# Attention and a mixture of experts on one core: the first expert's first range grows from 256 to 384 rows, and a batch's gating moves into the attention

## The chip, the cores and the metric

The kernel runs on one NeuronCore of a Trainium2 chip. The metric is the device time of one execution in microseconds (us); lower is better. The engines are TensorE (PE, with its weight loads shown as PEld), VectorE (DVE), ScalarE (ACT), GpSimd (POOL) and SyncE (SP, which only issues transfers).

## The reference

Three stages follow each other. Everything is float32.

```python
# attention: q, k, v of 4 batches x 8 heads x 576 positions x 64; a window of 64 positions
scores = where(0 <= rel < 64, scale * q @ k.T, -1e9); out = softmax(scores) @ v
x = out.transpose(0, 2, 1, 3).reshape(2304, 512)
# experts: 8 of them, each token goes to two
noisy = x @ w_gate + log1p(exp(x @ w_noise)) * noise
for the two largest of each row, with weights softmax(those two):
    out[row] += weight * (relu(x[row] @ w1[e]) @ w2[e])     # 512 -> 1024 -> 512
# a last dense layer on all rows: 512 -> 2048 -> 512
g = h * clip(h + 3, 0, 6) / 6 with h = out @ w_in;  result = g @ w_out
```

## The kernel before, in words

**Attention.** 16 pairs of heads (`n` = 0 to 15, four pairs to a batch), each in three groups of query chunks, are 48 steps `g` of one software pipeline. The order on TensorE is written by hand; DVE, ACT, POOL and SP are ordered by the scheduler when the program is built. A step turns the exponentials (`pt`), makes the scores (`s`) of a later group, and multiplies with the values (`pv`); DVE takes the maxima (`mx`) and writes the normalised rows to `xbuf` (`normalise`). `load_pair(n + 3)` fetches a later pair's q and k (`rq`, `rk`) and v; a transfer waits, on SP, for one issued eight before it.

**Gating.** The 2304 tokens are 18 tiles of 128; they become known batch by batch (`DONE`: tiles 0-3, 4-8, 9-12, 13-17). `gate_batch` gives a list of steps for one batch: `turn_tile` (four transposes of a tile, and its rows to DRAM, `x_rows`), `logits`, `logits_back`, `s1` to `s5` (the noise, the two largest, their one-hot masks `mk`, and each token's place in its expert's list), then per tile `runs` (two pairs of one-hot matrices `pa` and `pbt` on DVE) and `mms` (their products on TensorE), and `total`, which adds the products to the lists (`iacc`). In the attention these steps hang in the list `fill`, and `bg` places a few of them in each step `g`.

**The first expert early.** After `KNOWN` batches, `hold` copies the first columns of the lists to `idx0`; `gather(0, m)` fetches 128 rows each on POOL, and `build(0, m)` turns them (`xg` to `xh`, `xl`: each float32 matrix is a high and a low part, so one product is three matmuls). An expert works in two ranges of rows (`expert_sub(e, 0)` and `(e, 1)`): 8 column groups of hidden products `ph`, 12 matmuls each, then for each block of 128 rows 24 matmuls `py`. `put(f, ...)` hangs a step between these matmuls: the tables `when` and `when_late` hold the places, 0 to 31 behind each three `ph` matmuls, from 32 on behind each three `py` matmuls.

**Weights.** `Halves.step` loads a weight tile (`wraw`, two buffers), makes the high half (POOL or ACT), and one step later `settle` makes the low half on DVE. The first expert's eight tiles are stepped in the attention, at the end of pairs 5, 6, 7, 9, 10, 11, 13, 14 and 15; the second expert's in the first expert's second range.

Of the kernel before, what the change touches and what calls it, by code (L numbers as in the profile page):

```python
# [29 lines left out]
CAP = 5  # L30
LIM = CAP * 128
SUBS = ((0, 2), (2, CAP))

HOLD = SUBS[0][1] * 128
KNOWN = 2

BASE = 1024
NEG = -1.0e30
# [7 lines left out]
def attention_moe_kernel(ctx, tc, q, k, v, w_gate, w_noise, noise, w1, w2, w_in, w_out, out):  # L46
# [47 lines left out]
    first_part = gp.tile([128, 1], F32, name="first_part")  # L94
    dve.tensor_copy(first_part, ident[:, 0:1])

    idx0 = consts.tile([128, SUBS[0][1]], I32, name="idx0")
    idx4 = consts.tile([128, 4, E, CAP], I32, name="idx4")
    rows4 = consts.tile([128, 4, NT, 2], I32, name="rows4")
    gates4 = consts.tile([128, 4, NT, 2], F32, name="gates4")  # L100
# [219 lines left out]
    def gate_batch(ts, bank):  # L320
# [149 lines left out]
        if t0 + n == NT:  # L470
            chain = firsts + [logits, logits_back, s1, s1b, s2, s3, s3b, s4, s5]
            return (chain + [lambda i=i: runs(i) for i in range(n)] + [lambda i=i: mms(i) for i in range(n)] +
                    [total, weigh, piece_rows])
        chain = [("tr", f) for f in firsts] + [("col", logits)]
        chain += [(None, f) for f in (None, logits_back, s1, s1b, s2, s3, s3b, None, None, s4, None, s5)]
        for i in range(n):
# [2 lines left out]

    def hold():  # L480

        dve.tensor_copy(idx0, iacc[:, 0:SUBS[0][1]])
        pc = gps.tile([128, 512], F32, name="g")[:, 0:1]
        pe.matmul(pc, ones, macc[:, 0:1], start=True, stop=True)
        h = gp.tile([128, 1], F32, name="held")
        dve.tensor_scalar(h, pc, -1.0, float(HOLD), op0=OP.mult, op1=OP.add)
        dve.tensor_scalar(h, h, 0.0, first_part, op0=OP.max, op1=OP.mult)
        dve.tensor_tensor(macc[:, 0:1], macc[:, 0:1], h, op=OP.add)
# [12 lines left out]
    def gather(e, m):  # L501
        if e == 0:
            t = XG[e, m] = mp.tile([128, DM], F32, name="xg", bufs=4)
            early = m < SUBS[0][1]
# [34 lines left out]

    def build(e, m):  # L540
        if e == 0:
            s = int(m >= SUBS[0][1])
            turn_rows(XG[e, m], *columns(e, s), 128 * (m - SUBS[s][0]))
# [104 lines left out]
    fill, late, coming = [], [], []  # L648

    def bg(*kinds, n=1):  # L650

# [6 lines left out]
    with tc.manual_schedule(engines={mybir.EngineType.PE}):  # L658
        for which in ("rq", "rk"):
            for a in range(2):  # L660
                tr_half(0, which, a)
        scores(0)
        odd_slots(1)
        scores(1)
        exps(0)

        for g in range(NG + 2):
            n, j = divmod(g, 3)
            for past in ((g - 3, g - 2) if g > 2 and g % 2 else ()):
                normalise(past)  # L670
                m, jj = divmod(past, 3)
                b, p = divmod(m, HP)
                if p == HP - 1 and jj == 2 and b < B - 1:
                    t = gate_batch(DONE[b], lambda: gps.tile([128, 512], F32, name="g"))
                    if b == B - 2:
                        cut = [f for _, f in t].index(None) + 5
                        t, late = t[:cut], [f for _, f in t[cut:] if f]
                    coming += t
                    if b == KNOWN - 1:
                        coming += [(None, None), (None, hold)]  # L680
                        coming += [(None, lambda m=m: gather(0, m)) for m in range(SUBS[0][1])]
                        coming += [(None, None)] * 2
                        coming += [("tr", lambda m=m: build(0, m)) for m in range(SUBS[0][1])]
            bg(None, "tr" if j == 0 else None)
            if g < NG:
                transposes(g)
            if g + 1 < NG:
                exps(g + 1)
            if g < NG:
                pt_copy(g)  # L690
            if g == 0:
                for which in ("rq", "rk"):
                    for a in range(2):
                        tr_half(1, which, a)
            elif j:
                which = ("rq", "rk")[j - 1]
                tr_half(n + 2, which, 0)
                tr_half(n + 2, which, 1)
            if g + 2 < NG:
                scores(g + 2)  # L700
            if g and g % 2 == 0:
                values(g - 2, g - 1)
                bg("col", n=2)
            fill += coming
            del coming[:]
            bg(None, "tr")
            if j == n % 2:
                load_pair(n + 3)
                if n == 1:
                    for w, s in ((w_gate, 0), (w_noise, E)):  # L710
                        for a in range(4):
                            sp.dma_start(wg[:, a, s:s + E], ap_of(w, 32 * a * E, [[128 * E, 4], [E, 32], [1, E]]))
            if j == 2:
                odd_slots(n + 2)
                if n in (5, 6, 7, 9, 10, 11, 13, 14, 15):
                    w0q.step()
        while fill:
            bg(None, "tr", "col", n=len(fill))
    order = ctx.enter_context(ExitStack())
    order.enter_context(tc.manual_schedule())  # L720

# [146 lines left out]

    def expert_sub(e, s, at):

        m0, m1 = SUBS[s]


        if e == 0:
# [61 lines left out]
    NF = F2 // 128  # L936
    three = consts.tile([128, 1], F32, name="three")
    dve.memset(three, 3.0)
    Y, table = {}, None

    def fetch(t, i):

# [20 lines left out]
    for e in range(E):  # L963
# [6 lines left out]
        wq = Halves(expert_weights(e + 1) if e + 1 < E else w_ins + w_outs)  # L970
        if e == 0:
            t = gate_batch(DONE[B - 1], lambda: eps.tile([128, 512], F32, name="py", bufs=2))
            t += [lambda m=m: gather(0, m) for m in range(A1, M)] + [lambda m=m: build(0, m) for m in range(A1, M)]

            when = [0, 1, 3, 5, 7, 10, 12, 12, 13, 14, 16, 18, 28, 28, 30, 31, 31, 32, 33,
                    36, 37, 38, 39, 40, 40, 41, 44, 40, 40, 40, 45, 46, 47]
            when_late = [2, 3, 14, 14, 24, 24, 25, 26, 27, 30]
            assert len(when) == len(t) and len(when_late) == len(late)
            for i, f in list(zip(when_late, late)) + list(zip(when, t)):
# [18 lines left out]
        expert_sub(e, 0, at)  # L998

        at.clear()  # L1000
        if e == 0:
            gating.close()
            wpool[1] = pool_of(ctx, "w1")
            fourth.append(pool_of(ctx, "fourth", space=PSUM))
            narrow = ctx.enter_context(ExitStack())
            nar = pool_of(narrow, "narrow")
            wq.fetch()
            nq.fetch()
        elif 1 < e < 5:
            for f in range(8):  # L1010
                put(lambda: next(table, None), "f", f, 1)
        if e == 5:
            for _ in table:
                pass
        if e + 1 < E:
            for m, f, late in ((0, 0, ("f", 6, 0)), (1, 2, ("m", A1, 1)), (2, 4, ("m", A1 + 1, 0))):
                put(lambda m=m: gather(e + 1, m), "f", f, 0)
                put(lambda m=m: build(e + 1, m), *late)
            if e == 0:
                for key in (("f", 1, 1), ("f", 3, 0), ("f", 4, 1), ("f", 6, 1), ("m", A1, 1), ("m", A1, 3),  # L1020
                            ("m", A1 + 1, 2), ("m", A1 + 2, 1)):
                    put(wq.settle, *key)
            for key in ((("f", 1, 0), ("f", 2, 1), ("f", 4, 0), ("f", 5, 1), ("f", 7, 1), ("m", A1, 2),
                         ("m", A1 + 1, 1), ("m", A1 + 1, 3)) if e == 0 else
                        (("f", 1, 1), ("f", 5, 0), ("m", A1, 0), ("m", A1 + 1, 1), ("m", A1 + 2, 0))):
                put(wq.step, *key)
            if e:
# [226 lines left out]
```

## Time and profile before

| | us |
|---|---|
| three runs | 1005.97, 1006.91, 1008.25 (median 1006.91) |
| the profiled execution: its time | 1005.52 |
| its span | 1003.7 |
| TensorE busy | 981.5 (98%) |
| VectorE, ScalarE, GpSimd busy | 567.7, 465.5, 325.9 |
| attention, up to the first `ph` matmul | 0 to 131.88 |
| first expert, to the second's first `ph` matmul | 131.88 to 204.76 |
| experts 2 to 8 and the dense layer | the rest |

TensorE's busy time counts instructions that overlap, so 98% doesn't say that it ran at its peak; what it waited for is read from the gaps in its timeline, and its clock from the column PEclk (1.00 is 2.4 GHz, 0.50 is 1.2 GHz).

### The profile page before, as it was taken

What the parts mean: (1) busy time and instruction counts of PE and PEld (TensorE: products, weight loads), DVE (VectorE), ACT (ScalarE), POOL (GpSimd) and SP (SyncE); (2) the same over time, 40 slices, a digit from 0 to 9 for tenths busy, and PEclk for the clock granted to TensorE, in tenths of its full rate; (3) what the DMA queues carried; (4) which work ended last, traced back from release to release, by engine and by line L of the source; (5) the groups of instructions that cost most, each with busy time, mean ns of one, the idle gap of its engine ahead of it and who ended that gap; (6) DMA issues with size and microseconds to landing.
All of it is one profiled execution on the core that took longest, in us unless ns stands there. A gap on an engine that the chain in (4) does not pass through costs nothing.

```text
span 1003.7 us, 17393 instructions
## 1 busy us (share of the span) xinstructions
PE 981.5 (98%) x6422; PEld 890.8 (89%) x6422; DVE 567.7 (57%) x1398; ACT 465.5 (46%) x1034; POOL 325.9 (32%) x351
## 2 busy tenths in 40 slices
PE   8989989999999999999999999999999999999998
PEld 7988877998988989999998988989988998899997
DVE  5587974666777686666666656435233433344322
ACT  6877742444444444544454446434333433334333
POOL 2132203732425343232421276732344234410000
PEclk9999998999999999999999999999999999999999
DMA  9997432636666566656666463200111002100000
GB/s 170 188 230 196 120 117 69 188 122 202 202 185 205 183 184 186 201 171 207 201 202 198 150 204 117 70 23 27 48 32 48 24 25 64 28 27 22 11 11 24
DMA packets 116394, 122.42 MB, mean 122 GB/s; under 512 B 69840, under 2 KB 78288, under 8 KB 116304
## 3 DMA queue, kind: packets, MB, share of 16 engines
q1 hardware_dynamic: 96144, 86.17, 31.0%
q0 software_dynamic: 9488, 19.94, 7.1%
q10 hardware_dynamic: 10672, 15.15, 4.1%
q8 instruction: 51, 0.84, 0.3%
q14 instruction: 39, 0.32, 0.1%
HBM read 92.91 MB, written 28.31 MB: 121 GB/s over the span
## 4 chain that ended last, share of the span: by engine, by line
PE 86%; DVE 6%; DMA 3%; ACT 2%; issue 1%; SPq 0%; POOL 0%; ACTq 0%; DVEq 0%
PE ph L892 7%; PE ph L894 7%; PE ph L893 7%; PE ph L1193 6%; PE ph L1191 6%; PE ph L1192 6%; PE py L912 5%; PE py L914 5%; PE py L913 5%; PE py L1214 5%; PE py L1213 5%; PE py L1212 5%; PE s L239 2%; PE pv L285 2%; PE pt L255 2%; PE tr L1212 1%
## 5 line engine op out<-in xcount | busy, mean ns | idle before, releaser
L512 POOL DMA_INDIRECT xg<-x_rows,idx x140 | 145.8, 1041 | 221.3 <-DVE xt L523 169.4
L948 POOL DMA_INDIRECT xg<-y_rows,rows x144 | 144.9, 1006 | 222.0 <-DVE xg L956 77.0
L1196 DVE SCALAR_TENSOR_TENSOR g<-g,ph 128x384 f32<-128x384 f32 (+1 forms) x112 | 55.7, 497 | 158.7 <-ACT g L1195 154.6
L1195 ACT ACTIVATE g<-ph,three 128x384 f32<-128x384 f32 (+1 forms) x112 | 60.0, 536 | 100.7 <-PE ph L1193 97.7
L900 DVE SCALAR_TENSOR_TENSOR hl<-ph,hh 128x320 fp32r<-128x320 f32 (+2 forms) x128 | 61.0, 487 | 76.1 <-ACT hh L899 76.1
L1201 DVE TENSOR_TENSOR hl<-g,hh 128x384 fp32r<-128x384 f32 (+1 forms) x112 | 56.2, 502 | 58.9 <-ACT hh L1199 56.1
L899 ACT ACTIVATE hh<-ph 128x320 fp32r<-128x320 f32 (+2 forms) x128 | 54.3, 436 | 67.0 <-PE ph L894 63.8
L1199 ACT CAST hh<-g 128x384 fp32r<-128x384 f32 (+1 forms) x112 | 52.4, 467 | 63.8 <-DVE g L1196 63.8
L517 ACT CAST xh<-xt 128x512 fp32r<-128x512 f32 (+1 forms) x60 | 33.5, 570 | 81.7 <-DVE xt L523 81.3
L518 DVE TENSOR_TENSOR xl<-xt,xh 128x512 fp32r<-128x512 f32 (+1 forms) x60 | 37.2, 630 | 39.8 <-ACT xh L517 39.8
L247 ACT ACTIVATE pb<-s,mx 128x128 f32<-128x128 f32 x144 | 42.4, 369 | 10.7 <-DVE mx L241 7.2
L239 PE MATMUL s<-kt,qbd 128*128 128x128 f32 x288 | 39.9, 275 | 0.2 <-ACT kt L226 0.2
L239 PEld LDWEIGHTS s<-kt,qbd 128*128 128x128 f32 x288 | 38.4, 191 | 0.8 <-ACT kt L226 0.5
L241 DVE TENSOR_REDUCE mx<-s 128x3 f32<-128x384 f32 x48 | 26.6, 554 | 21.5 <-PE s L239 16.1
L523 DVE STREAM_TRANSPOSE xt<-xg 128x512 f32<-128x512 f32 x53 | 37.4, 706 | 0.4
L156 POOL TENSOR_SCALAR vt<-vt 64x520 f32<-64x520 f32 (+1 forms) x32 | 19.2, 600 | 53.4 <-DMA vt<-in_v_dram 30.2
L751 DVE SCALAR_TENSOR_TENSOR na<-mag,raw 128x256 f32<-128x256 f32 x64 | 26.8, 420 | 12.1 <-DMA w_out<-na 5.1
L748 ACT ACTIVATE mag<-raw 128x256 f32<-128x256 f32 x64 | 27.5, 430 | 12.5 <-DVE na L757 12.4
L757 DVE CUSTOM_DVE_ANT_0 na<-mag,nr 128x512 uint16<-128x512 uint16 x64 | 27.3, 426 | 9.1 <-DVE mag L756 0.5
L920 ACT COPY y<-py 128x512 f32<-128x512 f32 x33 | 19.3, 584 | 28.1 <-PE py L914 20.6
L756 DVE SCALAR_TENSOR_TENSOR mag<-na,mag 128x256 int32<-128x256 int32 x64 | 27.3, 426 | 2.2
L285 PE MATMUL pv<-vt,ptb 128*64 128x65 f32 x640 | 26.2, 225 | 2.2 <-DVE xbuf L304 2.2
(517 smaller groups left out, 3174.4 us busy)
## 6 DMA issues: line engine op xcount, KB each, us to landing
wraw<-in_moe_w_dram SPq DMA_DIRECT2D x60, 512.0 KB
y_rows<-y ACTq DMA_DIRECT2D x40, 256.0 KB
raw<-in_moe_w_in_dram SPq DMA_DIRECT2D x32, 256.0 KB
raw<-in_moe_w_out_dram SPq DMA_DIRECT2D x32, 256.0 KB
rq<-in_q_dram SPq DMA_DIRECT2D x32, 144.0 KB
rk<-in_k_dram SPq DMA_DIRECT2D x32, 144.0 KB
x_rows<-xbuf SPq DMA_DIRECT2D x18, 256.0 KB
out_dram<-y ACTq DMA_DIRECT2D x17, 256.0 KB
```

What stands on the lines that cost most here:

```text
L239: pe.matmul(s[:, i, :], l, KT[n][:, k0:k0 + 128], start=False, stop=(i == 2))
L512: pool.indirect_dma_start(out=t[:, i], out_offset=None, in_=pieces(xrows), in_offset=bass.IndirectOffsetOnAxis(ap=idx4[:, i, e, m:m + 1], ...
L892: pe.matmul(p, wh[:, fs], xh[:, d, :n], start=(d == 0), stop=False)
L893: pe.matmul(p, wh[:, fs], xl[:, d, :n], start=False, stop=False)
L894: pe.matmul(p, wl[:, fs], xh[:, d, :n], start=False, stop=(d == 3))
L900: dve.scalar_tensor_tensor(hl[f][:, cs], p, 0.0, hh[f].bitcast(F32)[:, cs], op0=OP.max, op1=OP.subtract)
L948: pool.indirect_dma_start(out=g[:, r], out_offset=None, in_=pieces(left), in_offset=bass.IndirectOffsetOnAxis(ap=rows4[:, r, tt, j:j + 1], ...
L1191: pe.matmul(p, wh[:, c], xh[:, d, :n], start=(d == 0), stop=False)
L1192: pe.matmul(p, wh[:, c], xl[:, d, :n], start=False, stop=False)
L1193: pe.matmul(p, wl[:, c], xh[:, d, :n], start=False, stop=(d == 3))
L1195: act.activation(g, p, AF.Relu, bias=three)
L1212: pe.matmul(py[i], gh[f][:, ms], wh[:, ws], start=(f == 0), stop=False)
```

## The change

The first expert's ranges are now 384 and 256 rows (`FIRST`), and `KNOWN` is 3, so the first range takes rows from tiles 0 to 12. The third batch's gating, of which steps from `s1` on stood between the first range's matmuls, now runs wholly in the attention, with several steps to a place; from pair 12 on each step `g` has one place more. Behind the attention stand the fourth batch's transposes and logits, what is left of `fill`, and the three builds, all ahead of the first range. The first expert's weights are stepped earlier, at pairs 2, 3, 4, 5, 8, 9, 10, 11 and 15. The second expert's weights start between the first range's `py` matmuls. Cut to its core:

```diff
+FIRST = ((0, 3), (3, CAP))
+HOLD = FIRST[0][1] * 128
+KNOWN = 3
...
+        if t0 + n == DONE[KNOWN][0]:
+            return ([("tr", f) for f in firsts] +
+                    [("col", logits)] + [(None, f) for f in (None, logits_back, lambda: (s1(), s1b()), s2,
+                                                             lambda: (s3(), s3b()), None, s4, None, s5,
+                                                             lambda: (runs(0), weigh()))] +
+                    [(None, lambda i=i: (mms(i - 1), runs(i))) for i in range(1, n)] + [(None, last)])
...
-                    if b == B - 2:
-                        cut = [f for _, f in t].index(None) + 5
-                        t, late = t[:cut], [f for _, f in t[cut:] if f]
...
+                        coming += [(None, hold), (None, lambda: [gather(0, m) for m in range(FIRST[0][1])])]
...
+            if n >= 4 * KNOWN:
+                bg(None)
...
-                if n in (5, 6, 7, 9, 10, 11, 13, 14, 15):
+                if n in (2, 3, 4, 5, 8, 9, 10, 11, 15):
                     w0q.step()
...
+            early = len(DONE[B - 1]) + 1
+            for f in t[:early]:
+                f()
+            while fill:
+                bg(None, "tr", "col", n=len(fill))
+            for m in range(FIRST[0][1]):
+                build(0, m)
...
+            t = t[early:] + [lambda m=m: gather(0, m) for m in range(FIRST[0][1], M)] + [change]
+            t += [lambda m=m: build(0, m) for m in range(FIRST[0][1], M)]
+            t += [wq.step, wq.settle] * 4
+            when = [2, 2, 4, 6, 8, 10, 16, 16, 20, 21, 22, 24, 25, 25, 27, 29, 31, 33, 33, 34, 36, 34, 34, 37, 44, 46,
```

TensorE's order from the last full set of value products to the first hidden product, before (`tr<-ident,xg` is a build, `tr<-ident,xbuf` a tile's transposes, `g<-xT,wg` the third batch's logits):

```order
L285 MATMUL pv<-vt_147,ptb 64x65 x14
L532 MATMUL tr<-ident,xg 128x128 x4
L255 MATMUL pt<-ident,pb 128x128 x3
...
L285 MATMUL pv<-vt_148,ptb 64x65 x12
L316 MATMUL tr<-ident,xbuf 128x128 x4
L338 MATMUL g<-xT,wg 32x128 x16
L892 MATMUL ph<-xh_2400,hwa 128x256
```

And in the change (`g<-mk` and `g<-macc` count places, `g<-pbt,pa` are the one-hot products, `py<-xT,wg` the fourth batch's logits):

```order
L286 MATMUL pv<-vt_147,ptb 64x65 x14
L339 MATMUL g<-xT,wg 32x128 x16
L348 MATMUL g<-ident,lt 128x128
...
L394 MATMUL g<-mk,before 128x8
L256 MATMUL pt<-ident,pb 128x128 x3
...
L431 MATMUL g<-pbt,pa 128x144
L317 MATMUL tr<-ident,xbuf 128x128 x8
L491 MATMUL g<-macc,ones 128x1
L317 MATMUL tr<-ident,xbuf 128x128 x12
L339 MATMUL py<-xT,wg 32x128 x16
...
L539 MATMUL tr<-ident,xg 128x128 x12
L893 MATMUL ph<-xh_2714,hwa 128x384
```

The whole of the third batch's lists, the three builds and the fourth batch's five tiles now stand between the attention's last full set of value products and the first hidden product; the third batch's own four tiles stand ahead of this piece.

DVE's order in the change, at the third batch's places in the last steps of the attention (`mk` the masks, `lza` the low half of the first expert's last weight tile, `posn` to `qf` the places):

```order
L385 TENSOR_TENSOR mk<-oh 128x32
L454 TENSOR_SCALAR gw<-gw 128x4
L397 TENSOR_REDUCE msum<-mk 128x8
...
L398 TENSOR_TENSOR macc<-macc,msum 128x8
L407 TENSOR_TENSOR oh<-oh,g 128x64
L592 TENSOR_TENSOR lza<-wraw,hza 128x1024
L408 TENSOR_REDUCE posn<-oh 128x8
...
L415 SCALAR_TENSOR_TENSOR qf<-blkn,posn 128x8
L423 TENSOR_SCALAR pbt<-iotab,cf,tokid 128x144 x2
L422 TENSOR_SCALAR pa<-iota_127,qf 128x128 x3
```

`lza` stood between normalisations before, and now stands inside the chain of the places. Behind the eight pairs of one-hot matrices come the last normalisations, then `iacc` and `idx0`.

SP's order from pair 5's loads on, in the change (`wraw` are quarter tiles of the first expert's weights; before, one `rq` of pair 6 stands where the first `wraw` stands here, and the rest of pair 6 and all of pair 7 where the seven stand):

```order
L170 DMA rq<-in_q_dram 96x6x64 x2
L170 DMA rk<-in_k_dram 96x6x64 x2
L574 DMA wraw<-in_moe_w_dram 32x1024
L173 DMA vt_146<-in_v_dram 128x4x64 x2
L175 DMA vt_146<-in_v_dram 64x2x64
L574 DMA wraw<-in_moe_w_dram 32x1024 x7
L170 DMA rq<-in_q_dram 96x6x64 x2
L170 DMA rk<-in_k_dram 96x6x64 x2
```

Pair 6's first load is now the sixteenth transfer from pair 5's first; it was the fifth.

## Rows read from the trace of the kernel before

**Rows 1.** The page: busy time of the engines.
```profile
PE 981.5 (98%) x6422; PEld 890.8 (89%) x6422; DVE 567.7 (57%) x1398; ACT 465.5 (46%) x1034; POOL 325.9 (32%) x351
```

**Rows 2.** Windows: stretch, length, busy of PE, PEld, DVE, ACT, POOL (instructions), PEclk, DMA, GB/s.
```profile
60.00:100.00 40.00, 35.99 (x496) 32.80 (x493) 32.88 (x120) 29.18 (x87) 11.42 (x16) 1.00 0.82 205
```

**Rows 3.** Windows of 2 us at and in the first range, same columns.
```profile
132.00:134.00 2.00, 2.00 (x18) 2.00 (x19) 0.28 (x1) 0.76 (x2) 0.00 (x0) 1.00 1.04 377
...
146.00:148.00 2.00, 0.43 (x4) 0.22 (x2) 1.93 (x14) 0.00 (x0) 0.00 (x0) 1.00 0.00 0
148.00:150.00 2.00, 1.43 (x8) 1.10 (x9) 1.93 (x12) 0.00 (x0) 0.00 (x0) 0.79 0.00 0
150.00:152.00 2.00, 2.00 (x24) 1.81 (x24) 1.73 (x9) 0.38 (x1) 0.00 (x0) 0.50 0.00 0
...
156.00:158.00 2.00, 2.00 (x11) 1.63 (x10) 0.00 (x0) 0.00 (x0) 0.00 (x0) 1.00 0.00 0
```

**Rows 4.** Timeline, PE, 121 to 205: start, length, instruction, idle before and what ended it.
```profile
121.52 1.15 PE L285 MATMUL pv<-vt,ptb 128*64 128x65 f32 x28
...
131.88 0.38 PE L892 MATMUL ph<-xh,hwa 128*128 128x256 f32 x1
...
148.05 0.61 PE L430 MATMUL g<-pbt,pa 128*128 128x144 f16 x2 [1.62 <-DVE pbt L422]
...
166.78 0.65 PE L532 MATMUL tr<-ident,xg 128*128 128x128 f32 x4 [0.61 <-DMA xg<-x_rows,idx]
...
171.82 0.45 PE L893 MATMUL ph<-xl,hwa 128*128 128x384 f32 x1 [0.28 <-DVE xl L518]
...
188.40 0.39 PE L912 MATMUL py<-hwb,hh 128*128 128x512 f32 x1
...
204.76 0.30 PE L892 MATMUL ph<-xh,hsa 128*128 128x320 f32 x1
```

**Rows 5.** Timeline, DVE and PE, 67 to 71.
```profile
67.15 1.22 DVE L585 TENSOR_TENSOR lxa<-wraw,hxa 128x1024 fp32r<-128x1024 f32 x1
70.67 0.69 PE L285 MATMUL pv<-vt,ptb 128*64 128x65 f32 x16 [1.60 <-DVE xbuf L304]
```

**Rows 6.** Timeline, SP's issues and PE's transposes of q, 28 to 40.
```profile
28.08 1.12 SPq L169 DMA_DIRECT2D rq<-in_q_dram  x2
37.51 1.43 SPq L567 DMA_DIRECT2D wraw<-in_moe_w_dram  x3
32.62 0.66 PE L212 MATMUL tr<-ident,rq 96*128 96x96 f32 x6
39.55 0.66 PE L212 MATMUL tr<-ident,rq 96*128 96x96 f32 x6
```

**Rows 7.** Timeline, PE, transposes of two tiles and a batch's logits.
```profile
50.31 1.08 PE L338 MATMUL g<-xT,wg 128*32 128x128 f32 x32
127.61 1.17 PE L316 MATMUL tr<-ident,xbuf 128*128 128x128 f32 x8
```

**Rows 8.** Timeline, DVE: the steps of a batch's gating.
```profile
52.17 0.19 DVE L354 TENSOR_SCALAR zc<-g 128x32 f32<-128x32 f32 x1 [0.42 <-PE g L347]
...
134.59 0.19 DVE L354 TENSOR_SCALAR zc<-g 128x32 f32<-128x32 f32 x1 [2.31 <-PE g L347]
...
138.83 0.19 DVE L384 TENSOR_TENSOR mk<-oh 128x32 f16<-128x32 f32 x1
...
141.90 0.16 DVE L397 TENSOR_TENSOR macc<-macc,msum 128x8 f16<-128x8 f16 x1
...
143.13 0.16 DVE L414 SCALAR_TENSOR_TENSOR qf<-blkn,posn 128x8 f32<-128x8 f32 x1
...
149.56 0.25 DVE L421 TENSOR_SCALAR pa<-iota,qf 128x128 f16<-128x128 f16 x1
...
149.95 0.25 DVE L421 TENSOR_SCALAR pa<-iota,qf 128x128 f16<-128x128 f16 x1
...
162.53 0.31 DVE L440 TENSOR_TENSOR iacc<-g,iacc 128x144 f32<-128x144 f32 x1 [0.83 <-PE g L430]
```

More of the change, by code (lines that the diff above doesn't have):

```diff
@@ L32 @@
 SUBS = ((0, 2), (2, CAP))
-HOLD = SUBS[0][1] * 128
-KNOWN = 2
+FIRST = ((0, 3), (3, CAP))
+HOLD = FIRST[0][1] * 128
+KNOWN = 3
 BASE = 1024
@@ L95, in attention_moe_kernel @@
     dve.tensor_copy(first_part, ident[:, 0:1])
-    idx0 = consts.tile([128, SUBS[0][1]], I32, name="idx0")
+    idx0 = consts.tile([128, FIRST[0][1]], I32, name="idx0")
     idx4 = consts.tile([128, 4, E, CAP], I32, name="idx4")
@@ L480, in hold @@
     def hold():
-        dve.tensor_copy(idx0, iacc[:, 0:SUBS[0][1]])
+        dve.tensor_copy(idx0, iacc[:, 0:FIRST[0][1]])
         pc = gps.tile([128, 512], F32, name="g")[:, 0:1]
@@ L503, in gather @@
             t = XG[e, m] = mp.tile([128, DM], F32, name="xg", bufs=4)
-            early = m < SUBS[0][1]
+            early = m < FIRST[0][1]
             ix = idx0[:, m:m + 1] if early else idx[:, e, m:m + 1]
@@ L541, in build @@
         if e == 0:
-            s = int(m >= SUBS[0][1])
-            turn_rows(XG[e, m], *columns(e, s), 128 * (m - SUBS[s][0]))
+            s = int(m >= FIRST[0][1])
+            turn_rows(XG[e, m], *columns(e, s), 128 * (m - FIRST[s][0]))
         elif m == 2:
@@ L647, in attention_moe_kernel @@
         pe.matmul(warm[:, 0:128], ones, ones, start=True, stop=True)
-    fill, late, coming = [], [], []
+    fill, coming = [], []
     def bg(*kinds, n=1):
@@ L674, in attention_moe_kernel @@
                     t = gate_batch(DONE[b], lambda: gps.tile([128, 512], F32, name="g"))
-                    if b == B - 2:
-                        cut = [f for _, f in t].index(None) + 5
-                        t, late = t[:cut], [f for _, f in t[cut:] if f]
                     coming += t
                     if b == KNOWN - 1:
[L680 to L683, printed above, removed]
+                        coming += [(None, hold), (None, lambda: [gather(0, m) for m in range(FIRST[0][1])])]
             bg(None, "tr" if j == 0 else None)
@@ L714, in attention_moe_kernel @@
                 odd_slots(n + 2)
-                if n in (5, 6, 7, 9, 10, 11, 13, 14, 15):
+                if n in (2, 3, 4, 5, 8, 9, 10, 11, 15):
                     w0q.step()
-        while fill:
-            bg(None, "tr", "col", n=len(fill))
     order = ctx.enter_context(ExitStack())
@@ L869, in expert_sub @@
     def expert_sub(e, s, at):
-        m0, m1 = SUBS[s]
+        m0, m1 = (SUBS if e else FIRST)[s]
         if e == 0:
@@ L938, in attention_moe_kernel @@
     dve.memset(three, 3.0)
-    Y, table = {}, None
+    Y, table, nar = {}, None, None
+    narrow = ctx.enter_context(ExitStack())
     def fetch(t, i):
@@ L972, in attention_moe_kernel, with change @@
             t = gate_batch(DONE[B - 1], lambda: eps.tile([128, 512], F32, name="py", bufs=2))
[L973 to L979, printed above, removed]
+            early = len(DONE[B - 1]) + 1
[5 more added lines that the diff above has]
+                build(0, m)
+            def change():
+                nonlocal nar
+                gating.close()
+                wpool[1] = pool_of(ctx, "w1")
+                fourth.append(pool_of(ctx, "fourth", space=PSUM))
+                nar = pool_of(narrow, "narrow")
+                wq.fetch()
+                nq.fetch()
+            t = t[early:] + [lambda m=m: gather(0, m) for m in range(FIRST[0][1], M)] + [change]
+            t += [lambda m=m: build(0, m) for m in range(FIRST[0][1], M)]
+            t += [wq.step, wq.settle] * 4
+            when = [2, 2, 4, 6, 8, 10, 16, 16, 20, 21, 22, 24, 25, 25, 27, 29, 31, 33, 33, 34, 36, 34, 34, 37, 44, 46,
+                    39, 41, 43, 45, 47, 49, 51, 53]
+            assert len(when) == len(t)
+            for i, f in zip(when, t):
                 put(f, *(("d", i // 4, i % 4) if i < 32 else ("s", (i - 32) // 8, (i - 32) % 8)))
@@ L1000, in attention_moe_kernel @@
         at.clear()
[L1001 to L1009, printed above, removed]
+        if 1 < e < 5:
             for f in range(8):
@@ L1015, in attention_moe_kernel @@
         if e + 1 < E:
-            for m, f, late in ((0, 0, ("f", 6, 0)), (1, 2, ("m", A1, 1)), (2, 4, ("m", A1 + 1, 0))):
+            a1 = A1 if e else FIRST[1][0]
+            for m, f, late in ((0, 0, ("f", 6, 0)), (1, 2, ("m", a1, 1)), (2, 4, ("m", a1 + 1, 0))):
                 put(lambda m=m: gather(e + 1, m), "f", f, 0)
@@ L1019, in attention_moe_kernel @@
             if e == 0:
-                for key in (("f", 1, 1), ("f", 3, 0), ("f", 4, 1), ("f", 6, 1), ("m", A1, 1), ("m", A1, 3),
-                            ("m", A1 + 1, 2), ("m", A1 + 2, 1)):
+                for key in (("f", 2, 1), ("f", 5, 0), ("f", 7, 1), ("m", 3, 3)):
                     put(wq.settle, *key)
-            for key in ((("f", 1, 0), ("f", 2, 1), ("f", 4, 0), ("f", 5, 1), ("f", 7, 1), ("m", A1, 2),
-                         ("m", A1 + 1, 1), ("m", A1 + 1, 3)) if e == 0 else
+            for key in ((("f", 1, 0), ("f", 3, 1), ("f", 6, 0), ("m", 3, 1)) if e == 0 else
                         (("f", 1, 1), ("f", 5, 0), ("m", A1, 0), ("m", A1 + 1, 1), ("m", A1 + 2, 0))):
```

## The prediction

> **What bounds the kernel now.** The page's row of busy times comes first [rows 1]: TensorE is at 98%, nothing else above 57%. That counts overlaps, so I went on to TensorE's own timeline between three marks [rows 4]. The attention's last full set of value products ends at 121.52 + 1.15 = 122.67. The first hidden product starts at 131.88, the second expert's first at 204.76. What follows 204.76 is the same work before and after the change; if all goes as below, its time moves as a block, and the result is what the change does to 204.76.
>
> Inside, TensorE loses time in three places. In the attention the windows from 60 to 100 show 35.99 busy of 40 [rows 2], so at most 4.0 are idle there; one such wait, 1.60 for `xbuf`, stands at 70.67, and DVE had `lxa`, 1.22, at 67.15 [rows 5]. In the first range TensorE waits 1.62 at 148.05 for the third batch's one-hot matrices [rows 4]. Around that wait it is busy 0.43 and 1.43 of two successive 2 us windows, and the granted clock goes to 0.79 and then to 0.50, that is 1.2 GHz of 2.4; it is back at 1.00 in the window from 156 [rows 3]. Against full clock this lost 0.21 x 2 = 0.42, and 0.5 x 6 = 3.0 from 150 to 156: 3.4 at most, of which I take 2.9, since short matmuls don't run at the rate of the clock. Third, from `iacc` at 162.53 (the fourth batch's lists done) to the second range's first product at 171.82 [rows 4, 8], gathers and builds of three blocks go one behind the other: 9.3.
>
> **The change part by part, in the attention.** The low halves on DVE leave the busy part around 60 to 68: the wait of 1.60 should go. I take -2.0 for this and its like; the ends are 0 (TensorE waits for something else) and -4.0 (all idle time there), the latter a rival.
>
> Pair 6's loads go behind the weights. Pair 5's first q load is issued at 28.08 and used at 32.62, so 4.5 or less from issue to use; pair 6's is now the sixteenth transfer from pair 5's first, and the sixteenth stood at 37.51 before [rows 6]. It then lands at 41 to 42, against a use at 39.55. So +2.0; ends 0 (it lands in 2.0) and +3.5 (each issue as long as the one at 37.51, 1.43). TensorE has nothing in store to make this up.
>
> The third batch's four tiles are transposed ahead of the mark now. Two tiles take 1.17 [rows 7], with gaps 4 x 0.55 = 2.2; some of it fills old waits, +1.5. The mark stands at 122.67 - 2.0 + 2.0 + 1.5 = 124.2. The attention's other pairs and queues stay; POOL's and ACT's high halves only move, to places where both have room.
>
> **The hand-over.** Behind the mark the third batch's logits (1.08) are made and everything up to the first hidden product is one chain. Logits to `zc`: 52.17 - 50.31 = 1.86 as in another batch [rows 7, 8]. `zc` to `mk`: 138.83 - 134.59 = 4.24 in the first range; maxima and normalisations now stand between, so 4.7 (ends 4.2 and 5.5): `mk` at 130.8. Counting: `mk` to `macc` took 3.07 with other work between, bare it is a few matmuls of eight columns; 0.65 taken (ends 0.2 and 3.07). `macc` to the end of `qf` 1.39. `lza` stands inside now, 1.2 as its equal `lxa` [rows 5]. Eight pairs of one-hot matrices, one each 149.95 - 149.56 = 0.39 [rows 8]: 3.1. The last normalisations before `iacc`, about one more such instruction, 1.0. Together 7.3: `iacc` at 138.1. Then three gathers and builds as after 162.53: 9.3, of which 9.0 taken, since `idx0` is three columns only. Ends 8.3 and 10.8: the upper one has the fourth batch's rows (five tiles of 256 KB) stand in front of the gathers at the 377 GB/s of the window 132 to 134 [rows 3], 3.4, half of it met. First hidden product near 147: **15.0 later** than 131.88.
>
> What hides the fourth batch's tiles and logits is this chain: TensorE has in those 23 us two batches' logits (1.1 and 1.4), five tiles (0.6 each) [rows 7], three builds (0.65 each), four tiles' one-hot products (0.61 each at most) [rows 4], and the last value products, some 2; together about 12. So they cost nothing, and leave it idle for half of the time.
>
> **First expert.** 384 rows: 16.6 for the hidden products (171.82 to 188.40) and 16.4 for `py` (188.40 to 204.76) [rows 4]. 256 rows: two thirds, 11.1 and 10.9; 0.2 more for the hidden ones, whose short matmuls gain less. The fourth batch's remaining steps stand between: two builds of 0.65 and five tiles' one-hot products, 0.3 to 0.61 each [rows 4]; 3.0 in all. Sum 58.2 against 204.76 - 131.88 = 72.88: **-14.7**. It holds what the old stage lost to waits, to the clock, and to the third batch's pieces. It assumes that the fourth batch's one-hot matrices and the second range's gathers are ready at their places; by the durations above there is about 1 us in hand at either.
>
> **Second expert's weights earlier.** At 204.76 TensorE doesn't wait [rows 4], so this brings nothing. It costs nothing while the second half of the `py` matmuls covers it; uncovered, a low half of 1.2 [rows 5] stands before the second range's builds.
>
> **Clock.** In the new hand-over TensorE works about half the time, as it did in the 4 us before 150, with one gap near 2.6 (1.39 + 1.2) between the counts and the first one-hot products. I expect the clock to go to 0.50 there, and the first range to start with it: +2.9, as measured there; ends 0 and 3.4.
>
> **Sum**: +15.0 - 14.7 + 2.9 = +3.2. On the profiled execution's own 1005.52 this is 1008.7; it lies 1.39 under the median, 1006.91, so the forecast is **1010.1**.
>
> **What the skill adds.** The trace has the clock at 0.50 behind the windows at 0.43 and 1.43 of 2 busy [rows 3]. The Trainium skill, "TensorE: Matmul & The Clock Gate", Part 1, says that activity releases the throttle, that idleness brings it back to half rate, and (Terms) that the penalty is throttled time x (1 - K/N); the trace agrees, by which 6.8 us at half rate lose an estimated 3.4, and the sum would be +3.7 instead of +3.2.
>
> **Rivals.**
> *The clock stays at 1.00.* For it: the fourth batch's five tiles and logits are spread through the hand-over, where the old stretch had one bare wait. Against: half of the time is still idle. It decides by the granted clock from 131 to 150. Without the 2.9 the result is +0.3, 1007.2: no change, so not slower.
> *DVE's relief is worth all idle time of 60 to 100* [rows 2]: 2.0 more, +1.2, 1008.1. For it: `lxa` is right in front of the only wait of that size. Against: other waits there are short and not behind weights.
> *The fourth batch's one-hot matrices come late*, at a place like 148.05: a second wait of 1.62 and a second fall of the clock, 2.9, so +7.7, 1014.6. It decides when the places' last step on DVE comes later than about 1 us behind my time.
> *The chain is shorter*: `mk` at its 4.2, last normalisations behind `iacc`, gathers at 8.3: 0.5 + 1.0 + 0.7 = 2.2 earlier, +1.0, 1007.9. With the clock at 1.00 too, -1.9; with DVE's relief besides, faster, 1003.
>
> **How the numbers follow.** Forecast 0.48 (own range 1006.5 to 1013.5, from the ends of the loads, the gathers and the clock); clock stays 0.22; DVE's relief and shorter chain 0.08 each; late one-hot matrices 0.08; anything else 0.06. The range goes from the rivals joined (1004) to the late matrices (1014.6). 0.2%, 2.0 us, is about what a measurement of this kernel can tell from no change. Above 1008.9 lie some two thirds of the forecast, a third of three rivals, and the late matrices: 0.54. Below 1004.9 lie the joined rivals and the forecast's lower tail: 0.16. The rest, 0.30, is no change.
>
> **What the new profile would show.** No wait near 70 for `xbuf`; a wait of TensorE for `rq` near 40, of about 2; the first hidden product some 15 later, with gaps in TensorE's row before it that end on DVE's one-hot matrices and on gathers; `lza` between the masks and `qf`; granted clock under 1.00 at the first range's start; no wait like 148.05's in the first range; none for gathers between the ranges, nor at the second expert's start; that start about 3 later than 204.76. I am wrong if the hand-over takes 12 or 18 instead of 15, if the clock holds, or if a wait stands inside the first expert.

## The result, and the profile after

The changed kernel takes 1015.5 us (median of 4 runs, 1014.62 to 1016.93), the kernel before 1006.66 (median of 4): 1.0087 times, interval 1.0069 to 1.0105. Slower was right, the size was not: +8.8 where +3.2 was forecast, and 1015.5 lies above the range's end of 1014.6.

The page, busy time of the engines (answers to [rows 1]):

```profile
PE 984.8 (97%) x6422; PEld 894.3 (88%) x6422; DVE 566.3 (56%) x1398; ACT 465.1 (46%) x1034; POOL 328.4 (32%) x351
```

TensorE has the same number of instructions and is 3.3 us busier; the engines' shares tell nothing about where the time went. The timeline of TensorE in the changed kernel (start, length, instruction, idle before and what ended it), as [rows 4]:

```profile
124.36 1.15 PE L286 MATMUL pv<-vt,ptb 128*64 128x65 f32 x28
...
131.82 0.17 PE L394 MATMUL g<-mk,before 128*128 128x8 f16 x1 [1.27 <-DVE mk L385]
...
135.30 1.22 PE L431 MATMUL g<-pbt,pa 128*128 128x144 f16 x4 [2.63 <-DVE pa L422]
...
144.79 0.63 PE L539 MATMUL tr<-ident,xg 128*128 128x128 f32 x4 [0.93 <-DMA xg<-x_rows,idx]
149.47 1.09 PE L539 MATMUL tr<-ident,xg 128*128 128x128 f32 x4 [4.05 <-DMA xg<-x_rows,idx]
150.98 1.09 PE L539 MATMUL tr<-ident,xg 128*128 128x128 f32 x4 [0.42 <-DMA xg<-x_rows,idx]
152.75 0.69 PE L893 MATMUL ph<-xh,hwa 128*128 128x384 f32 x1 [0.68 <-ACT xh L524]
...
173.92 0.48 PE L913 MATMUL py<-hwb,hh 128*128 128x512 f32 x1
...
214.13 0.30 PE L893 MATMUL ph<-xh,hsa 128*128 128x320 f32 x1
```

One wait is new in kind: 4.05 us for the second gathered block, with 0.42 for the third. DVE's timeline gives the chain of the lists (answers to [rows 8]):

```profile
127.30 0.19 DVE L355 TENSOR_SCALAR zc<-g 128x32 f32<-128x32 f32 x1 [0.42 <-PE g L348]
...
131.57 0.19 DVE L385 TENSOR_TENSOR mk<-oh 128x32 f16<-128x32 f32 x1
...
132.53 1.23 DVE L592 TENSOR_TENSOR lza<-wraw,hza 128x1024 fp32r<-128x1024 f32 x1
...
134.42 0.16 DVE L415 SCALAR_TENSOR_TENSOR qf<-blkn,posn 128x8 f32<-128x8 f32 x1
...
138.81 0.30 DVE L441 TENSOR_TENSOR iacc<-g,iacc 128x144 f32<-128x144 f32 x1
```

The marks beside the forecast (us; the first hidden product is 131.88 + 15.0 in the forecast's sum, 146.9; its terms, 138.1 + 9.0, give 147.1, so the 15.0 is 0.2 short of them):

| | before | forecast | after | length of the piece: forecast, after |
|---|---|---|---|---|
| end of the last full set of value products | 122.67 | 124.2 | 125.51 | |
| `iacc`, third batch | | 138.1 | 138.81 | 13.9, 13.3 |
| first hidden product | 131.88 | 146.9 | 152.75 | **9.0, 13.9** |
| second expert's first hidden product | 204.76 | 208.0 | 214.13 | 61.1, 61.4 |
| end of the span | 1003.7 | | 1013.1 | |

What the texts call the last full set of value products is followed by one more of 28 matmuls, at 125.70 before and at 128.68 after; the mark is the same set, the third from the end, in both.

From the second expert on the two are alike (1003.7 - 204.76 = 798.9, 1013.1 - 214.13 = 799.0), so all of the 9.4 in the profile arises before. Of the 6.2 that the forecast missed, 4.9 lie in one piece, from `iacc` to the first hidden product; 1.3 in the attention.

What runs there is seen on POOL's timeline (the gathers' issues) and SP's (start and length of the issuing, number of transfers) of the changed kernel:

```profile
140.19 1.14 POOL L513 DMA_INDIRECT xg<-x_rows,idx  x1 [31.77 <-DVE xbuf L305]
141.63 0.96 POOL L513 DMA_INDIRECT xg<-x_rows,idx  x1 [0.30 <-issue]
142.90 0.95 POOL L513 DMA_INDIRECT xg<-x_rows,idx  x1 [0.31 <-issue]
```

```profile
138.40 3.44 SPq L314 DMA_DIRECT2D x_rows<-xbuf  x5
141.93 1.53 SPq L578 DMA_DIRECT2D wraw<-in_moe_w_dram  x2
143.72 0.80 SPq L739 DMA_DIRECT2D raw<-in_moe_w_in_dram  x2
```

The view of the transfers of the same kernel, 136 to 152 (KB each; for `xg` the median us from issue to landing):

```profile
x_rows<-xbuf SPq DMA_DIRECT2D x5, 256.0 KB
wraw<-in_moe_w_dram SPq DMA_DIRECT2D x2, 512.0 KB
raw<-in_moe_w_in_dram SPq DMA_DIRECT2D x2, 256.0 KB
xg<-x_rows,idx POOLq DMA_INDIRECT x3, 6.1
```

The trace has the landing of the first two gathers only, 4.5 and 7.7 us after their issue, and 6.1 is the middle of these two; the third gather's rows are used from 150.98 on, 8.1 after its issue.

Windows of 2 us there (length, busy of PE, PEld, DVE, ACT, POOL, PEclk, DMA, GB/s):

```profile
134.00:136.00 2.00, 0.61 (x3) 0.31 (x3) 1.93 (x12) 0.00 (x0) 0.00 (x0) 0.57 0.00 0
...
144.00:146.00 2.00, 0.63 (x4) 0.42 (x4) 0.35 (x1) 0.54 (x1) 0.00 (x0) 1.00 0.96 379
146.00:148.00 2.00, 0.00 (x0) 0.00 (x0) 0.69 (x1) 0.04 (x1) 0.00 (x0) 0.99 0.95 354
148.00:150.00 2.00, 0.53 (x3) 0.56 (x4) 0.00 (x0) 0.00 (x0) 0.00 (x0) 0.50 0.99 384
...
154.00:156.00 2.00, 2.00 (x8) 2.00 (x7) 0.00 (x0) 0.00 (x0) 0.00 (x0) 0.50 0.00 0
...
158.00:160.00 2.00, 2.00 (x13) 2.00 (x12) 1.25 (x4) 0.73 (x2) 0.00 (x0) 0.95 0.00 0
```

From 144 to 150 the transfer engines are 95% busy and more. The three gathers share them with nine transfers of SP: 5 x 256 + 2 x 512 + 2 x 256 KB, 2.9 MB. The forecast had five of them. The other four are the second expert's first two weight tiles and two pieces of the last layer's weights. SP's timeline of the kernel before has the same nine:

```profile
129.96 2.41 SPq L313 DMA_DIRECT2D x_rows<-xbuf  x5
132.46 1.64 SPq L571 DMA_DIRECT2D wraw<-in_moe_w_dram  x2
139.46 0.80 SPq L738 DMA_DIRECT2D raw<-in_moe_w_in_dram  x2
```

There they lay beside hidden products, with the first range's gathers long done and the next at 163. In the program the four stand behind the first range (before) or between its products (after), but they wait only for a buffer, and SP issues the first two right behind the row writes (138.40 + 3.44 = 141.84, then 141.93).

The granted clock, as in [rows 3]: 0.57 in the window from 134, with TensorE busy 0.61 of 2; 1.00 again in the window from 144; 0.50 in the window from 148, behind one in which it did nothing. The first range begins at 0.50.

### The profile page after: what moved, and what is told of

Same layout as the page of the kernel before. It is cut to its first block, busy times and chain, and to the rows that moved or that the text cites. A ratio compares the mean times of both kernels' runs of the same rounds, so it can differ in the third digit from the quotient of the medians.

```text
span 1013.1 us, 17388 instructions
## 1 busy us (share of the span) xinstructions
PE 984.8 (97%) x6422; PEld 894.3 (88%) x6422; DVE 566.3 (56%) x1398; ACT 465.1 (46%) x1034; POOL 328.4 (32%) x351
## 4 chain that ended last, share of the span: by engine, by line
PE 86%; DVE 6%; DMA 4%; ACT 2%; issue 1%; SPq 1%; POOL 0%; ACTq 0%; DVEq 0%
PE ph L893 7%; PE ph L894 7%; PE ph L895 7%; PE ph L1204 6%; PE ph L1202 6%; PE ph L1203 6%; PE py L913 5%; PE py L914 5%; PE py L915 5%; PE py L1225 5%; PE py L1224 5%; PE py L1223 5%; PE s L240 2%; PE pv L286 2%; PE tr L1224 1%; PE tr L1225 1%
## 5 line engine op out<-in xcount | busy, mean ns | idle before, releaser
L519 POOL DMA_INDIRECT xg<-x_rows,idx x140 | 147.9, 1056 | 216.4 <-DVE xt L530 164.9
L242 DVE TENSOR_REDUCE mx<-s 128x3 f32<-128x384 f32 x48 | 26.6, 553 | 25.9 <-PE s L240 20.5
L261 ACT COPY ptb<-pt 128x384 f32<-128x384 f32 x48 | 23.2, 484 | 11.1 <-PE pt L256 11.0
```

## The experiments

They ran in four groups (a group is what the expectations name a call), each on one chip with 35 runs of the kernel before beside it, which there takes 1029 to 1046 us in the median instead of 1006.66. So the times in the expectations can't be compared, only ratios within a group, and lengths of stages in profiles. The first group has the first run on the transfers, the first with rows and weights behind the gathers, the one with 44 matmuls of no use and the one with the old steps: the changed kernel itself didn't run in it, nor in the third, so its ratio beside those runs is one of another group. How the kernels behave differently there is shown with the control runs.

**Is it the transfers beside the gathers?** The theory, A: the transfers that SP starts delay the gathers. The rival, B: three gathers queued behind each other are slow by themselves. In the first run the four weight transfers wait for the third gather, by a column of it copied into their buffers; the two weight tiles' loads are called right behind the builds:

```diff
+            if self.key in (("w1", 1, 0), ("w1", 1, 1)):
+                pool.tensor_scalar(o[:, 0:1], XG[0, 2][:, 0:1], 1.0, 0.0, op0=OP.mult, op1=OP.add)
...
+            if self.src is w_in and self.c < 2:
+                dve.tensor_copy(self.raw[:, 0:1, 0].bitcast(F32), XG[0, 2][:, 0:1])
...
+            wq.fetch()
```

> The changed kernel, but the second expert's first two weight tiles and the last layer's first two pieces (1.57 MB) may only start once the third gather has landed (a one-column copy from the gathered block into each buffer). Theory A, the first range's gathers share the transfer engines with what SP starts at the same time: from iacc to the first hidden product 11 to 11.5 us instead of 13.9, time 1012.5 to 1013. Rival B, the gathers are slow by themselves (three queued one behind the other, behind the third batch's row writes): 13.9 stays, time 1015.5.

In the second the fourth batch's rows wait too (`LATE` holds their five writes, which `turn_tile` no longer issues):

```diff
+            xs = xbuf[:, DONE[B - 1][0] % (NT // 2):DONE[B - 1][-1] % (NT // 2) + 1, 0, 0, 0]
+            dve.scalar_tensor_tensor(xs, XG[0, 2][:, 0:5], 0.0, xs, op0=OP.mult, op1=OP.add)
+            for a in LATE:
+                sp.dma_start(*a)
```

> As the run above, and the fourth batch's five row writes (1.28 MB) also wait for the third gather. Theory A: iacc to the first hidden product 9 to 9.5 us, as in the kernel before, time 1010 to 1011.5. Rival B: 13.9 stays, time 1015.5. If A is right but only the weights matter, this run equals the one above.

TensorE's timeline with the weights behind the gathers (`iacc` at 138.45), and then with rows and weights behind them (`iacc` at 141.37):

```profile
145.18 0.63 PE L539 MATMUL tr<-ident,xg 128*128 128x128 f32 x4 [1.38 <-DMA xg<-x_rows,idx]
146.65 1.26 PE L539 MATMUL tr<-ident,xg 128*128 128x128 f32 x8 [0.85 <-DMA xg<-x_rows,idx]
148.59 0.64 PE L897 MATMUL ph<-xh,hwa 128*128 128x384 f32 x1 [0.68 <-ACT xh L524]
```

```profile
147.85 0.63 PE L542 MATMUL tr<-ident,xg 128*128 128x128 f32 x4 [0.63 <-DMA xg<-x_rows,idx]
149.34 0.63 PE L542 MATMUL tr<-ident,xg 128*128 128x128 f32 x4 [0.87 <-DMA xg<-x_rows,idx]
150.65 0.45 PE L900 MATMUL ph<-xh,hwa 128*128 128x384 f32 x1 [0.67 <-ACT xh L527]
```

The wait of 4.05 is gone in the first. From `iacc` to the first hidden product: 13.9 in the changed kernel (13.2 and 12.6 in the controls below), 10.1 without the weights beside it (11 to 11.5 expected), 9.3 without the rows either. From the first gather's start to the first hidden product it is 12.6 in the changed kernel (140.19 to 152.75), 8.8 and 7.9 in these two (from 139.83 and 142.74), and 7.7 for the three gathers of the kernel before (163.37 to 171.09). With nothing beside it the second gather's rows are used 3.65 after its issue (144.20 to 147.85), against 7.84 in the changed kernel (141.63 to 149.47). A holds, B falls; taken out first, the weights are three quarters to four fifths of it. Ratios to the kernel before: 1.0018 (0.9992 to 1.0044) and 0.9992 (0.9973 to 1.0011). That the time follows is shown only by the repeat below, with the changed kernel in its group.

**Controls and repeats.** The changed kernel in the second and the fourth group, and the kernel before in the third:

> The changed kernel once more, as the measure for the other runs of this call. The first comparison gave 1.0087 times the kernel before; 1.007 to 1.0105 again.

1.0041 (1.0011 to 1.0072): less than expected.

> The kernel before once more, for its profile beside the other profiles of this call. Ratio 1.000. If the changed kernel's later start in the first 20 us (21.64 against 20.08 for the fourth transposes of q) belongs to the change, this run shows 20.1 again; if it belongs to the execution, 21.3 to 22.9 as the other runs.

0.998 (0.9952 to 1.0008): so far from 1 a kernel can come out against itself. The fourth transposes of q stand at 21.44: the late start belongs to the execution. In this profile of the kernel before the second expert starts at 215.50, not 204.76. Its windows, with TensorE's timeline in the second of them and the start of the second expert:

```profile
160.00:180.00 20.00, 17.36 (x95) 13.74 (x93) 5.47 (x18) 4.06 (x7) 12.98 (x14) 1.00 0.33 99
180.00:200.00 20.00, 13.33 (x56) 11.67 (x57) 6.19 (x9) 5.28 (x9) 5.00 (x6) 0.74 0.25 72
```

```profile
184.40 0.48 PE L893 MATMUL ph<-xl,hza 128*128 128x384 f32 x1 [1.70 <-issue]
185.82 0.48 PE L894 MATMUL ph<-xh,lza 128*128 128x384 f32 x1 [0.93 <-issue]
187.21 0.48 PE L892 MATMUL ph<-xh,hwa 128*128 128x384 f32 x1 [0.91 <-issue]
...
215.50 0.30 PE L892 MATMUL ph<-xh,hsa 128*128 128x320 f32 x1
```

TensorE is busy 13.33 of 20, and the gaps between its products there end on nothing that the profile shows ("issue"); from 184.40 to 188.61 a matmul starts only each 1.40 us, with a weight load half-way between two. From the first hidden product to the second expert's this kernel takes 83.5 instead of 72.9, 10.6 more, and with the new weight steps (below) 82.1; the changed kernel takes 66.2 and 66.7 in its controls instead of 61.4, 4.8 and 5.3 more. So the changed kernel looks better here, by about 5 us, than in the result. The second expert starts 4.3 and 3.9 later than in this profile of the kernel before, against 9.4 in the result, which is near what the ratios say; but the profiles are of different chips, one execution each. Most of the longer time comes behind this stage, in both kernels (824.2 from the second expert on in this profile, against 798.9). What the engine waits for isn't settled.

> The changed kernel, beside its three parts on one chip. Ratio to the kernel before 1.004 to 1.009; 13 to 14 us from iacc to the first hidden product.

1.0027 (1.0002 to 1.0052); from `iacc` (140.18) to the first hidden product (152.75) 12.6, and 13.2 in the first control: both a little less than expected.

> Weights and row writes behind the third gather, once more. If the stages of the profile add up in the time: 4.5 to 5 us (0.0045) less than the changed kernel in this call. If something later takes it back: less than 2 us less.

0.9978 (0.9957 to 0.9998): 0.0049 less than the changed kernel beside it, 5.1 us, and the two intervals don't meet; 9.3 from `iacc`, 3.3 less than beside it. The stage's gain arrives in the time; that the time gains more than the stage is within the intervals.

**The last low half in the chain.** The step of the first expert's last tile at pair 13 instead of 15, alone:

```diff
-                if n in (2, 3, 4, 5, 8, 9, 10, 11, 15):
+                if n in (2, 3, 4, 5, 8, 9, 10, 11, 13):
```

> The changed kernel with only the first expert's last weight step at pair 13 instead of 15, so that the last low half leaves the chain of the places. If the chain sets the first hidden product: 1.2 less than the changed kernel. Rival: the gathers then start 1.2 earlier but land no earlier, since the transfers in front of them are released by the same low half, which is earlier too: 0 to 3 less.

0.9992 (0.997 to 1.0015). As the changed kernel didn't run beside it, once more:

> The low half at pair 13 alone: by the profile of its first run 2 us (0.002) less than the changed kernel in this call; if its first ratio (0.9992) was its own and not the chip's, 5 us or more less, and the collision then is not what it cures.

1.001 (0.9986 to 1.0034), 0.0017 or 1.8 us less than the changed kernel of that group, within both intervals. The second gather is still waited for by 3.59 here: it cures the chain, not the collision. Beside the changed kernel of its group, `iacc` comes 1.1 sooner behind the attention (12.2 against 13.3), but from there to the first hidden product it takes 1.1 more (13.6 against 12.6), as in the rival above; in the first of the two runs this piece is 12.7, so one profile doesn't settle it. With everything behind the gathers as well (the "run above" of this expectation is the one with fewer matmuls of no use, under the clock):

> As the run above without the matmuls of no use: 5.5 us less than the changed kernel, ratio 1.003; the clock at 0.50 for some 4 us at the start of the first range.

0.9984 (0.995 to 1.0018), where the changed kernel had 1.0041: 0.0057 or 5.9 us less, as expected; the ratio lies lower than the 1.003, since the changed kernel's does.

> The run with everything behind the gathers and the low half at pair 13 once more, against the kernel before on another chip: ratio 0.9984 in the first, 0.996 to 1.003 expected; the stretch from the last full set of value products to the first expert's first output products 41.8.

0.9976 (0.9948 to 1.0004). The stretch took 42.9, not 41.8: the hidden products took 21.7 instead of 20.5, with the clock at 0.50 from 150 to 154.

> The same with the last low half at pair 13: 5.5 to 6 us (0.0055) less than the changed kernel in this call, ratio to the kernel before 0.998 to 1.003.

0.9995 (0.9969 to 1.0021): 0.0032 less than the changed kernel instead of 0.0055, and against 0.0049 for the run without the low half moved. So the low half shows in the stage (from the last full set of value products to the first hidden product 21.3 in three profiles, against 22.6 in the two without it) and isn't told apart in the time. These versions undo the loss; that they beat the kernel before is not shown, since only one interval of five ends below 1.

**The clock.** Matmuls of no use, 44 ahead of the first one-hot products and 24 ahead of each build:

```diff
+        def warm_up():
+            for i in range(44):
+                pe.matmul(lg[0][:, 0:128], ones, ones, start=True, stop=True)
...
+        for a in range(24 if c0 + 128 <= HOLD and len(XG) <= FIRST[0][1] else 0):
+            pe.matmul(tr[:, 0], ones, ones, start=True, stop=True)
```

> The changed kernel with matmuls of no use in the hand-over: 44 of 128 columns ahead of the first one-hot products and 24 ahead of each of the first range's builds. If the clock's fall after the idle stretches is what makes the first range start at 1.2 GHz: granted clock 1.00 from 134 on, first column groups at full speed, time 1012 to 1013. Rival: the fall is hidden behind the gathers and the fillers delay the builds by about 1.4 us: time 1014.5 to 1016.

Its windows in the hand-over, and its first output product (first hidden product at 156.20):

```profile
134.00:138.00 4.00, 2.81 (x53) 2.71 (x53) 3.86 (x27) 0.69 (x2) 0.00 (x0) 1.00 0.00 0
...
150.00:154.00 4.00, 2.90 (x40) 2.71 (x41) 0.69 (x1) 0.80 (x2) 0.00 (x0) 1.00 0.84 328
```

```profile
175.25 0.48 PE L919 MATMUL py<-hwb,hh 128*128 128x512 f32 x1
```

The clock stays at 1.00, and the first range's hidden products take 19.05 instead of 173.92 - 152.75 = 21.17: the fall costs 2.1 there. But from `iacc` to the first hidden product it took 14.8, and the ratio is 1.0051 (1.0019 to 1.0083), no better than the changed kernel's 1.0027 and 1.0041 in other groups. With fewer of them (30, and 8 ahead of each build) on top of the other two cures:

> The changed kernel with weights and row writes behind the gathers (4.0 to 4.7 us by the profiles of the first two runs), the last low half taken out of the chain of the places (step at pair 13 instead of 15: 1.2), and 30 plus 3 x 8 matmuls of no use that hold the clock (1.5 to 2.1). If the three costs add up: 7 us less than the changed kernel, ratio to the kernel before 1.001 to 1.002. Rival, the clock doesn't matter once the gathers are quick: as the run without fillers, within 0.5 us.

1.0015 (0.9983 to 1.0047), against 0.9984 beside it without them, and 0.0026 less than the changed kernel where 7 us were expected. The clock is 0.58 from 134 to 138 and 0.99 or more from there. From the last full set of value products to the first output product both take 41.8: hidden products 1.5 quicker, and begun 1.5 later. The fillers stand in front of what they are to speed up; that they cost time in all is not shown, since the intervals overlap.

**The first expert's weights.** The changed kernel with the old steps, and the kernel before with the new ones:

```diff
-                if n in (2, 3, 4, 5, 8, 9, 10, 11, 15):
+                if n in (5, 6, 7, 9, 10, 11, 13, 14, 15):
```

> The changed kernel with the first expert's weight steps at the old pairs. The prediction's terms: the relief of 2.0 near 70 is lost, the late loads of pair 6 (0.4 measured, 2.0 forecast) too, so the end of the attention's last full set of value products comes 0 to 1.6 later, time 1015.5 to 1017. Rival: the relief near 70 is given back by 105 (by then the changed kernel was level with the kernel before), time 1015.5 or up to 1 less.

1.0042 (1.0016 to 1.0068). The last full set of value products ends at 126.48; in the controls, with the new steps, at 127.16 and 126.88. The wait of 1.60 is back, at 72.41.

> The kernel before, with only the first expert's weight steps at the new pairs. The prediction's terms: relief -2.0 and late loads +2.0, and the low half that now stands in the attention's last steps: 0 in all, ratio 1.000. Rival: the late loads are only 0.4, the relief stays, ratio 0.998. Other rival: the low half in the last steps delays the first range, 1.001.

1.004 (1.0006 to 1.0073). The early steps bring nothing that these runs show in either kernel, and alone they may cost: in the second of these kernels the last full set ends at 126.24, against 122.47 in the other profile of the kernel before. The wait of 1.60 near 70 leaves with them; but there a wait of 1.07 for ACT stands at 71.84, and on TensorE's timeline a like one for `xbuf` later:

```profile
101.30 0.68 PE L285 MATMUL pv<-vt,ptb 128*64 128x65 f32 x12 [1.34 <-DVE xbuf L304]
```

**The second expert's weights.** The run with both cures, but these weights stepped in the second range alone, as before the change:

```diff
-            t += [wq.step, wq.settle] * 4
...
-            for key in ((("f", 1, 0), ("f", 3, 1), ("f", 6, 0), ("m", 3, 1)) if e == 0 else
+            for key in ((("f", 1, 0), ("f", 2, 1), ("f", 4, 0), ("f", 5, 1), ("f", 7, 1), ("m", 3, 1), ("m", 3, 3), ("m", 4, 2)) if e == 0 else
...
```

> As the run with everything behind the gathers and the low half at pair 13, but the second expert's eight weight tiles stepped in the first expert's second range alone, as before the change. The prediction's term for moving them earlier is 0. Rival: the second range now has 256 rows instead of 384, some 25 us instead of 50, and the eight tiles don't fit: a wait at the second expert's start, 3 to 10 more than that run.

1.0045 (1.0016 to 1.0074) against 0.9976 (0.9948 to 1.0004) beside it, 0.0069 or 7.2 us more. TensorE's timeline has two waits, of which the second answers to the expectation:

```profile
193.34 0.58 PE L900 MATMUL ph<-xh,hwa 128*128 128x256 f32 x1 [4.52 <-ACT xh L527]
...
220.30 0.41 PE L900 MATMUL ph<-xh,hsa 128*128 128x320 f32 x1 [1.93 <-ACT xh L527]
```

The first, at the second range's start, isn't explained by the edit: ACT, which ended it, had itself stood for 9.34, until something that the profile marks only as "remote". So the time is shown to be lost, and a wait at the second expert's start too; the 1.93 are only part of the 7.2, and where the rest is lost isn't shown.

## Why the prediction was wrong

**The step that failed** is the hand-over's last term: "Then three gathers and builds as after 162.53: 9.3, of which 9.0 taken", with the upper end 10.8 for "the fourth batch's rows (five tiles of 256 KB) ... half of it met". It measured 13.9 (13.2 and 12.6 in the controls). The mechanism was named, the list of transfers was short: four transfers, 1.6 MB, run in the same 10 us. With them out 10.1, inside the forecast's ends; with the rows out too 9.3. The row writes, which I did count, cost 0.9, half of what the bound had. The 377 GB/s by which I priced them were themselves these transfers: at 132 to 134 of the kernel before SP's row writes of 129.96 and the two weight tiles of 132.46 are on the way. The paragraph on the second expert's weights failed with it: "It costs nothing while the second half of the `py` matmuls covers it" looked at the steps' places in the program, not at when SP issues their loads. The sign that I had named came: the first hidden product is 20.9 later, not 15.

The 9.3 was also misread: 171.82 is the second range's second product. TensorE's timeline of the kernel before has the first one ahead of it:

```profile
171.09 0.44 PE L892 MATMUL ph<-xh,hwa 128*128 128x384 f32 x1 [0.68 <-ACT xh L517]
```

So the three gathers and builds took 8.6 there, and 384 rows' hidden products 17.3 instead of 16.6; in the sum the two slips nearly cancel. Of the 0.7 between 8.6 and the 9.3 measured with nothing beside the gathers, 0.5 stand between `iacc` and the first gather (1.37, against 0.84 before), which waits for a normalisation (`xbuf`) on DVE.

**The rest of the hand-over was right.** `zc` to `mk` 4.3 (4.7 forecast), `mk` to `iacc` 7.2 (7.3), with `lza` 1.23 inside and the wait of 2.63 (2.6) for the one-hot matrices. `iacc` came 0.7 late, from the attention.

**The attention** ends 2.8 later than before, 1.5 forecast; it ends at 125.1 to 128.9 in all profiles of the changed order (127.16 and 126.88 in the controls, 4.4 to 4.7 later than before), against 122.67 and 122.47 in those of the kernel before; why it spreads so isn't settled. Relief and late loads were to cancel at 2.0. The wait near 70 went, though in the controls one of 0.9 for ACT stands at 71; the late q of pair 6 was waited for by 0.21 only (0.48 and 1.71 in others); but a wait of 0.81 for ACT at 45.17 is new. The two runs on the steps agree that nothing is won here. The third batch's four tiles cost about 2.5, measured from the same step to the mark, from 101.58 before (21.1) and from 101.95 after (23.6); 1.5 was forecast, 2.2 the bare price: no old wait was filled.

**The first expert** took 61.4, 61.1 forecast. No wait like 148.05's stands in the first range, and none at the second expert's start, as forecast. **The clock** fell as forecast, behind stretches in which TensorE did little (0.61 of 2 us from 134, nothing from 146 to 148); with 44 and 24 matmuls of no use in them it stayed at 1.00. Its price was 2.1 in the first range, 2.9 forecast. By the Trainium skill, "TensorE: Matmul & The Clock Gate" (Terms), half of the throttled time is lost; from 152.75 to about 158.2, where the window's 0.95 has it back, that is an estimated 2.7, against the 2.1 measured between two profiles, and the measurement decides.

**The rivals.** None of them was this one. The late one-hot matrices gave nearly the right total, 1014.6, with a wait that isn't there. The term of 0 for the second expert's weights was right: TensorE doesn't wait at the second expert's start before (204.76) or after (214.13). But the move is needed, since without it the time is 7.2 us longer. In the later groups the ratio, 1.0041 and 1.0027, lies near the 1.0032 that was forecast. That is luck: the gathers are late there too, the attention ends later still, and the kernel before takes 10.6 more for its first expert, with gaps that weren't forecast.

## What to carry to other kernels

A load that waits for a buffer and not for its place runs when the queue comes to it: ahead of moving a gather on the path, list what the other queues issue in the same ten microseconds, from their timelines, and not what the program writes beside it. The same transfers can be harmless in one place and dear in another: beside hidden products TensorE was busy 2.00 of 2 us ([rows 3], 132 to 134), and beside gathers the nine cost 3 to 5 us. A cheap cure here was a data dependence on the urgent transfer, one column wide: the other transfers then waited until it had landed.

## What was not expected of the hardware

Of three gathers of 256 KB the first landed 4.5 us after its issue and the second 7.7, when 2.9 MB ran beside them at 354 to 384 GB/s; with nothing beside them the second's rows were used after 3.65. And the same kernel before took 1006.7 us in the result and 1029 to 1046 in the four later groups, with gaps of TensorE in the first expert's second range that have no releaser in the profile. By the profiles these gaps cost the two kernels unequally, and the change's ratio was 1.0087 in the result and 1.0041 and 1.0027 later; that the one explains the other is argued from single profiles, and whether the chip makes the difference isn't shown.
